# Sketched attention and a SwiGLU block on one core: other chunks of the output product in parts, alternating accumulator banks, and the main sum copied out one unit ahead

## The chip, the core and the metric

One core of a Trainium2 chip runs the whole program. The metric is the device time of one execution in microseconds (us), and for several runs their median. The engines, as the profile names them: PE is the matrix engine and PEld its weight loads, DVE the vector engine, ACT the scalar engine, POOL GpSimd, SP the engine that issues most of the DMAs.

## The reference

Inputs are float32. Attention comes first, with polynomial features of two small sketches; its output, heads side by side, is the input of a SwiGLU block.

```python
# q, k, v: (4, 4, 1088, 32)  S1, S2: (8, 32)
phi(x) = outer(S1 x, S2 x)                    # 64 features
kv = sum over s of phi(k) v;  z = sum over s of phi(k)
attn = (phi(q) kv) / (phi(q) z + 1e-6)
x = attn as (4352, 128)
g = x @ w_gate;  val = x @ w_val              # (4352, 1536)
out = (g * sigmoid(g) * val) @ w_out          # (4352, 128)
```

## The kernel before, in words

**Blocks and chunks.** The 4352 tokens are cut into ten blocks (`blocks`, L65 to L72): blocks 0 to 2 are batch 0 (384, 384 and 320 tokens), blocks 3 to 8 have 480 tokens and block 9, the last, has 384. The 1536 hidden channels are 12 chunks (NCH) of 128. A unit (i, j) is chunk j of block i: its gate and value products, SiLU, and the product of the two, the hidden tile. The down product adds, for each block, 12 chunks of hidden times w_out into one bank of PSUM, and `store` (L1091) turns the sum by 32x32 squares on DVE and sends it out with DMAs on SP's queue.

**The main loop.** Blocks 3 to 9 (`line`, L887) are 84 units, run by the loop at L1339 with y as the unit's number; in these texts block 3 + k, chunk j is written k.j, so y = 12k + j. Attention of the later batches is a generator (`attentions`, L608), advanced by `parts_of` once a unit up to y = 19; its groups of matmuls stand at y = 4, 6, 20, 22 and 40 (`GROUPS`). Every engine runs its instructions in the order in which the code issues them. Nothing reorders them, so the order of the calls is the schedule.

**Products in parts.** From block 3 on, a product is made from two parts of each operand: `cut_unit` (L959) multiplies a difference part into one bank (L968), and the main parts into another (L978, L979). ACT copies the first with a scale (L972) to SBUF, and DVE adds the second to it (L980, `sum`). Up to y = 19 only the value product is made so; from y = 20 (`GATES`) both are, side by side in a pair of banks. SiLU (L986) and POOL's product (L991) of a unit are then issued one unit late, by `finish`.

**Parts of tokens.** `cut_tokens` (L867) makes the parts of a block of tokens: x1 on ACT (L875) and x0 on POOL (L876) in its first step, xd on DVE (L880) in its second. `token_steps` (L1329) says at the end of which unit each step is issued. Block 3 + m needs them from y = 12m.

**The down product in parts.** Blocks 6, 7 and 8 (`line[3:6]`) multiply every third chunk (`DOWN`, L888) in parts as well: `cut_hidden` (L929) makes h1 on ACT, h0 on POOL and hd on DVE (L945), 2, 3 and 4 units after the unit. `down` (L1039) then issues three matmuls (L1052 into the block's bank, L1054 and L1055 into a second bank, "p"), where a plain chunk takes one matmul (L1058, in two passes). The other chunks of these blocks use w_out scaled by -4096 (`scaled`), so that the whole sum is p (1 + 1/4096) - d / 4096, where d is the block's bank. `put_together` (L1068) makes it: an ACT copy of d one unit after the block's last chunk, a DVE sum of the two after two units, the store after three. `before` and `behind` hold such steps by unit: `before` is run after a unit's ACT copy, `behind` after SiLU of the unit before it; both stand ahead of the unit's own `sum`.

**Banks and the queue of downs.** PSUM has 8 banks. Bank 3 ("acc") is held back all the time, bank 2 ("g2") from y = 20 on; the other six are taken as three pairs in turn, two pairs a unit. d of blocks 5 to 9 lies in g2, p always in acc. Units that are done wait in `todo`; `down` is called when it holds more than 5, or more than 6 ahead of the first chunk of blocks 4 and 7 to 9 (`wait`, L1352). So at y = 54, 66 and 78 there is no down, and at y = 55, 67 and 79 there are two.

Of the kernel before, what the change touches and what calls it, by code (L numbers as in the profile page):

```python
# [7 lines left out]
FP32 = mybir.dt.float32  # L8
# [4 lines left out]
AF = mybir.ActivationFunctionType  # L13
ALU = mybir.AluOpType
# [5 lines left out]
def kernel(  # L20
# [28 lines left out]
    nc = tc.nc  # L49
    P = nc.NUM_PARTITIONS  # L50
# [8 lines left out]
    NCH = Dff // P  # L59
# [11 lines left out]
    WB = 480  # L71
# [12 lines left out]
    fpool = ctx.enter_context(tc.tile_pool(name="ffn", bufs=2))  # L84
# [13 lines left out]
    def touch(*which):  # L98
        for i in which:
            clock[0] += 1  # L100
            used[i] = clock[0]
# [11 lines left out]
    def bank(tag=None):  # L113

        if tag is not None:
            i = place[tag]
        elif oldest[0]:
            i = min((i for i in used if i not in held), key=used.get)
        else:
            i = place[free_banks[turn[0] % len(free_banks)]]  # L120
            turn[0] += 1
        touch(i)
        return PS[:, i, :]
# [21 lines left out]
    wo = const.tile([P, NCH, D], FP32, name="wo")  # L145
# [32 lines left out]
    def load_next():  # L178
# [36 lines left out]
        out=ident[:], in_=ident[:], pattern=[[-1, P]], base=0, channel_multiplier=1,  # L215
# [583 lines left out]
    acc = {}  # L799
    todo = []  # L800
# [9 lines left out]
    BETA = 4096.0  # L810
# [4 lines left out]
    def whole(ap):  # L815
        return ap.bitcast(FP32)
# [50 lines left out]
    def cut_tokens(i, engine=nc.gpsimd):  # L867

        t0, n = blocks[i]
        x = xT[:, t0 : t0 + n]  # L870
        x1, x0, xd = x_parts[i] = [
            apool.tile([P, WB], F32R, tag=tag, name=name, bufs=2)
            for tag, name in (("qb", "x1"), ("dT", "x0"), ("rd", "xd"))
        ]
        nc.scalar.activation(x1[:, 0:n], x, AF.Copy, scale=CUT)  # L875
        engine.tensor_tensor(  # L876
            out=x0[:, 0:n], in0=x, in1=whole(x1[:, 0:n]), op=ALU.subtract
        )
        yield
        nc.vector.scalar_tensor_tensor(  # L880
            out=xd[:, 0:n], in0=whole(x0[:, 0:n]), scalar=-BETA, in1=whole(x1[:, 0:n]),
            op0=ALU.mult, op1=ALU.add,
        )
# [1 line left out]


    line = list(range(HEAD, len(blocks)))  # L887
    DOWN = [(i, j) for i in line[3:6] for j in range(2, NCH, 3)]  # L888
    down_parts = {}
    h_parts = {}  # L890
    h_sets = []
    before, behind = {}, {}

    def add_to(where, y, f):
        where.setdefault(y, []).append(f)
# [5 lines left out]
    def cut_down():  # L901

        n = NCH // 3
        parts = const.tile([P, 3, n, D], F32R, tag="late", name="dparts", bufs=1)
        w1, wb, wd = (parts[:, k] for k in range(3))
        scaled = apool.tile([P, n, 2, D], FP32, tag="zs", name="scaled")
        low = [apool.tile([P, 2, D], FP32, tag=tag, name="low" + tag)[:] for tag in ("kas", "kab2")]
        down_parts.update(w1=w1, wb=wb, wd=wd, scaled=scaled)
        third = wo[:, 2::3, :]
        others = wo[:].rearrange("p (c t) d -> p c t d", t=3)[:, :, 0:2, :]  # L910
        cs = [slice(c, c + 2) for c in range(0, n, 2)]
        nc.scalar.activation(w1, third, AF.Copy, scale=CUT)
        yield
        for c, x in zip(cs, low):
            nc.gpsimd.tensor_tensor(
                out=x, in0=third[:, c], in1=whole(w1[:, c]), op=ALU.subtract
            )
            yield
        for c, x in zip(cs, low):
            nc.scalar.activation(wb[:, c], x, AF.Copy, scale=BETA)  # L920
        yield
        for c in cs:
            nc.gpsimd.tensor_tensor(
                out=wd[:, c], in0=whole(w1[:, c]), in1=whole(wb[:, c]), op=ALU.subtract
            )
            yield
        nc.scalar.activation(scaled[:], others, AF.Copy, scale=-BETA)
# [31 lines left out]
    def cut_unit(i, j, both=False, y=None):  # L959
# [24 lines left out]
        def last():  # L984
# [6 lines left out]
            nc.gpsimd.tensor_tensor(out=hj[:, 0:n], in0=sg, in1=sums[:, len(ws) - 1], op=ALU.mult)  # L991
            if (i, j) in DOWN:
                cut_hidden(y, i, j)
# [45 lines left out]
    def down(y=None):  # L1039

        i, j = todo.pop(0)
        n = SPLIT if i == LAST else blocks[i][1]
        if j == 0:
            acc[i] = bank("g1" if i == 1 else "g2" if i in line[2:] else "acc")
        mine = [c for c in range(NCH) if (i, c) in DOWN]
        if mine and j == mine[0]:
            acc[i, "p"] = bank("acc")
        sides = dict(start=(j == 0), stop=(j == NCH - 1))
        if j in mine:
            w1, wb, wd = [down_parts[x][:, j // 3, :] for x in ("w1", "wb", "wd")]  # L1050
            h1, h0, hd = h_parts.pop((i, j))
            nc.tensor.matmul(acc[i][:, 0:n], wd, hd, **sides)  # L1052
            p = acc[i, "p"][:, 0:n]
            nc.tensor.matmul(p, w1, h1, start=(j == mine[0]), stop=False)  # L1054
            nc.tensor.matmul(p, wb, h0, start=False, stop=(j == mine[-1]))  # L1055
        else:
            w = down_parts["scaled"][:, j // 3, j % 3, :] if mine else wo[:, j, :]
            nc.tensor.matmul(acc[i][:, 0:n], w, hidden[i, j][:, 0:n], **sides)  # L1058
        if i != LAST:
            hidden.pop((i, j))  # L1060
            slots.append(slot_of[i, j])
        if j == NCH - 1:
            if mine:
                put_together(y, i, n)
            else:
                store(i, n)

    def put_together(y, i, n):  # L1068

        s = fpool.tile([P, WB], FP32, tag="sg", name="sum2", bufs=5)[:, 0:n]  # L1070
        d, p = acc.pop(i)[:, 0:n], acc.pop((i, "p"))[:, 0:n]
        acc[i] = s
        add_to(behind, y + 1, lambda: nc.scalar.activation(s, d, AF.Copy, scale=-1.0 / BETA))
        add_to(before, y + 2, lambda: nc.vector.scalar_tensor_tensor(
            out=s, in0=p, scalar=1.0 + 1.0 / BETA, in1=s, op0=ALU.mult, op1=ALU.add
        ))
        add_to(before, y + 3, lambda: store(i, n))

    def straight(ps, j):

# [10 lines left out]
    def store(i, n):  # L1091
        t0 = blocks[i][0]

        o = fpool.tile([P, WB // 32, 32], FP32, tag="o", name="o", bufs=2)
        nc.vector.transpose(
            out=o[:, 0 : n // 32, :], in_=acc.pop(i)[:, 0:n].rearrange("p (x t) -> p x t", t=32)
        )
        t1 = t0 + n
        while t0 < t1:
            b, x0 = divmod(t0 // 32, NX)  # L1100
            m = min(t1 - t0, S * (b + 1) - t0) // 32
            k = (t0 - blocks[i][0]) // 32
            for a in range(4):
                queue = nc.scalar if i == LAST and a % 2 else nc.sync
                queue.dma_start(
                    out=rows[b, a, :, x0 : x0 + m, :],
                    in_=o[32 * a : 32 * a + 32, k : k + m, :],
                )
            t0 += 32 * m
# [18 lines left out]
    for h in range(H):  # L1128
# [13 lines left out]
        out=s12[:],  # L1142
        in0=sTv.unsqueeze(1).to_broadcast([P, H, 2, R]),
        in1=own[:].unsqueeze(2).unsqueeze(3).to_broadcast([P, H, 2, R]),
# [20 lines left out]
    n = steps[0][1]  # L1165
# [58 lines left out]
    def group():  # L1224
        while ahead[0] != "pe":
            ahead[0] = next(att)
        ahead[0] = next(att, "end")
# [32 lines left out]
    w = ("wg", "wv")  # L1260
# [10 lines left out]
    for z, (i, j) in enumerate(seq):  # L1271
# [16 lines left out]
        if z == 20:  # L1288
# [4 lines left out]
            first, low, second, third = cut_weights(wv, lows, nc.gpsimd)  # L1293
# [32 lines left out]
    END = len(line) * NCH  # L1326
# [2 lines left out]
    token_steps = {}  # L1329
    for m, i in enumerate(line[1:], 1):  # L1330
        gen = cut_tokens(i)
        for at in {2: (20, 22), 4: (40, 43)}.get(m, (NCH * m - 9, NCH * m - 7 if m > 3 else NCH * m - 4)):
            token_steps.setdefault(at, []).append(gen)
    oldest[0] = True
    hold("acc")
# [3 lines left out]
    for y in range(END):  # L1339
        i, j = line[y // NCH], y % NCH  # L1340
        if y in GROUPS:
            group()
        if y == GATES:
            hold("g2")
        if y == END - 1:
            finish()
            unit(i, j)
        else:
            cut_unit(i, j, both=y >= GATES, y=y)
        for _ in range(2):  # L1350

            wait = todo[0][1] == 0 and todo[0][0] in line[1:2] + line[4:]  # L1352
            if len(todo) > min(5 + wait, END - y + 1):
                down(y)
        parts_of(y < GATES or y % 2 == 0)
        if y == 0:
            gate_rows = cut_weights(wg, lows, nc.vector)
        for n, row in enumerate(gate_rows):
            if y >= (0, 2, 6, 6)[n]:
                take(row, 1)  # L1360
        for gen in token_steps.get(y, ()):
            next(gen, None)
        if y in range(24, 38, 2):
            next(down_steps, None)
# [43 lines left out]
```

## Time and profile before

| | |
|---|---|
| median of 5 runs | 287.66 us (287.48 to 288.49) |
| the profiled execution's own time | 287.73 us |
| its span (first to last instruction) | 286.0 us |
| granted PE clock | 1.0 throughout |
| busy: DVE / ACT / POOL | 221.0 / 175.2 / 176.4 us |
| plain down chunk, 480 tokens, on PE | 0.81 us |
| DVE `sum` of a unit, one product / both | 0.65 / 1.16 us |
| DVE xd (L880), 7 times | 0.65 to 1.65 us |
| POOL product of a unit (L991), 480 tokens | 1.21 us at the shortest |
| DVE sum in `put_together` (L1074), 3 times | 0.64 us |
| ACT copy in `put_together` (L1073), 3 times | 0.57 us |

Times in the views count from the span's start. The main loop begins with the matmul at 93.26 us, y = 20 is at about 140 us, y = 54 at 218, y = 66 at 244, y = 78 at 268. "Idle before" in brackets is the time for which an engine stood still ahead of an instruction, with what released it.

### The profile page before, as it was taken

What the parts mean: (1) busy time and instruction counts of PE and PEld (TensorE: products, weight loads), DVE (VectorE), ACT (ScalarE), POOL (GpSimd) and SP (SyncE); (2) the same over time, 40 slices, a digit from 0 to 9 for tenths busy, and PEclk for the clock granted to TensorE, in tenths of its full rate; (3) what the DMA queues carried; (4) which work ended last, traced back from release to release, by engine and by line L of the source; (5) the groups of instructions that cost most, each with busy time, mean ns of one, the idle gap of its engine ahead of it and who ended that gap; (6) DMA issues with size and microseconds to landing.
All of it is one profiled execution on the core that took longest, in us unless ns stands there. A gap on an engine that the chain in (4) does not pass through costs nothing.

```text
span 286.0 us, 5579 instructions
## 1 busy us (share of the span) xinstructions
PE 278.3 (97%) x2129; PEld 190.8 (67%) x2129; DVE 221.0 (77%) x324; ACT 175.2 (61%) x316; POOL 176.4 (62%) x173
## 2 busy tenths in 40 slices
PE   8899999999999999999999999999999999999995
PEld 7545565666665675655676767757777677778884
DVE  3997988975595977999658889649887987888751
ACT  3568665723401857555276786867788688877760
POOL 3315432279500895499735878649979678888560
PEclk9999999999999999999999999999999999999999
DMA  6474194222321133001000020002000200020021
GB/s 199 153 217 115 55 263 138 80 78 80 89 33 28 26 91 83 2 0 26 12 16 0 1 34 2 0 2 34 0 0 1 36 1 0 1 37 1 0 34 28
DMA packets 26138, 14.28 MB, mean 50 GB/s; under 512 B 19840, under 2 KB 24192, under 8 KB 26112
## 3 DMA queue, kind: packets, MB, share of 16 engines
q1 hardware_dynamic: 25456, 13.84, 18.8%
q8 instruction: 16, 0.26, 0.4%
q10 hardware_dynamic: 656, 0.10, 0.2%
q14 instruction: 10, 0.08, 0.1%
HBM read 11.41 MB, written 2.23 MB: 48 GB/s over the span
## 4 chain that ended last, share of the span: by engine, by line
PE 86%; DVE 7%; ACT 2%; issue 2%; DMA 1%; SPq 0%; DVEq 0%; ACTq 0%
PE PS L1058 24%; PE PS L1015 16%; PE PS L968 10%; PE PS L978 10%; PE PS L979 10%; PE PS L970 5%; DVE sum L980 2%; PE PS L776 2%; PE PS L335 2%; PE PS L347 1%; DMA kld<-in_k_dram 1%; PE PS L381 1%; PE PS L1081 1%; ACT sum L972 1%; PE PS L1055 1%
## 5 line engine op out<-in xcount | busy, mean ns | idle before, releaser
L991 POOL TENSOR_TENSOR hbuf<-sg,sum 128x480 f32<-128x480 f32 (+1 forms) x83 | 105.2, 1272 | 39.9 <-ACT sg L986 32.5
L980 DVE SCALAR_TENSOR_TENSOR sum<-PS,sum 128x960 f32<-128x960 f32 (+2 forms) x83 | 83.3, 1004 | 29.9 <-ACT sum L972 24.0
L972 ACT ACTIVATE sum<-PS 128x960 f32<-128x960 f32 (+2 forms) x83 | 71.0, 855 | 39.1 <-PE PS L968 37.2
L1058 PE MATMUL PS<-hbuf,wo 128*128 128x480 f32 (+3 forms) x142 | 57.5, 506 | 0.0
L968 PE MATMUL PS<-xd,gphq 128*128 128x480 f32 (+1 forms) x63 | 39.1, 620 | 1.2 <-DVE sum L980 0.7
L978 PE MATMUL PS<-x,w 128*128 128x480 f32 (+1 forms) x83 | 38.5, 464 | 0.0
L986 ACT ACTIVATE sg<-sum 128x480 f32<-128x480 f32 (+1 forms) x63 | 36.7, 582 | 2.9 <-DVE sum L980 2.8
L968 PE MATMUL PS<-xd,wd 128*128 128x480 f32 (+1 forms) x83 | 35.8, 432 | 0.5 <-DVE xd L880 0.5
L1058 PEld LDWEIGHTS PS<-hbuf,wo 128*128 128x128 f32 x142 | 26.5, 189 | 8.7 <-issue 0.9
L979 PE MATMUL PS<-x,wb 128*128 128x480 f32 (+1 forms) x83 | 31.2, 376 | 0.0
L1015 PE MATMUL PS<-xT,wg 128*128 128x384 f32 (+1 forms) x74 | 29.5, 480 | 0.0
L1015 PE MATMUL PS<-xT,wv 128*128 128x384 f32 (+1 forms) x74 | 28.8, 471 | 0.2 <-DVE wv L279 0.2
L1019 ACT ACTIVATE sg<-PS 128x384 f32<-128x384 f32 (+1 forms) x31 | 14.4, 467 | 21.3 <-PE PS L1015 19.6
L968 PEld LDWEIGHTS PS<-xd,wd 128*128 128x128 f32 x83 | 15.7, 189 | 12.7 <-issue 11.3
L978 PE MATMUL PS<-x,graw 128*128 128x480 f32 (+1 forms) x63 | 23.8, 378 | 0.2 <-ACT xT L793 0.2
L979 PE MATMUL PS<-x,graw 128*128 128x480 f32 (+1 forms) x63 | 23.3, 371 | 0.0
L1058 PE MATMUL PS<-hbuf,scaled 128*128 128x480 f32 x48 | 23.1, 570 | 0.0
L968 PEld LDWEIGHTS PS<-xd,gphq 128*128 128x128 f32 x63 | 11.9, 188 | 12.3 <-issue 6.6
L1015 PEld LDWEIGHTS PS<-xT,wv 128*128 128x128 f32 x74 | 13.8, 190 | 9.2 <-DVE hbuf L1030 0.9
L1015 PEld LDWEIGHTS PS<-xT,wg 128*128 128x128 f32 x74 | 13.3, 189 | 9.3 <-issue 1.2
L978 PEld LDWEIGHTS PS<-x,w 128*128 128x128 f32 x83 | 15.6, 188 | 5.8 <-issue 3.2
L979 PEld LDWEIGHTS PS<-x,wb 128*128 128x128 f32 x83 | 15.6, 188 | 5.7 <-issue 4.3
(173 smaller groups left out, 457.3 us busy)
## 6 DMA issues: line engine op xcount, KB each, us to landing
kld<-in_k_dram SPq DMA_DIRECT2D x4, 544.0 KB, 4.1
vld<-in_v_dram SPq DMA_DIRECT2D x12, 144.0 KB, 5.5
qld<-in_q_dram SPq DMA_DIRECT2D x3, 544.0 KB, 3.5
raw<-in_moe_w_out_dram SPq DMA_DIRECT2D x4, 384.0 KB, 4.7
raw<-in_moe_w_gate_dram SPq DMA_DIRECT2D x3, 384.0 KB, 3.2
raw<-in_moe_w_val_dram SPq DMA_DIRECT2D x3, 384.0 KB, 3.4
out_dram<-o SPq DMA_DIRECT2D x16, 60.0 KB, 2.0
vld<-in_v_dram SPq DMA_DIRECT2D x4, 112.0 KB, 4.3
```

Source lines behind the costliest of these rows:

```text
L335: nc.tensor.matmul(ps[32 * a : 32 * a + 32, 96 * (c - c0) : 96 * (c - c0) + 96], qT[:, 4 * c + a, :], s123[:, a : a + H, :, :].rearrange(" ...
L968: nc.tensor.matmul(ds[:, k], wd, xd, start=True, stop=True)
L970: nc.tensor.matmul(g, wg[:, j, :], xT[:, t0 : t0 + n], start=True, stop=True)
L972: nc.scalar.activation(sums, ds, AF.Copy, scale=-1.0 / BETA)
L978: nc.tensor.matmul(ps[:, k], w1, x1, start=True, stop=False)
L979: nc.tensor.matmul(ps[:, k], wb, x0, start=False, stop=True)
L980: nc.vector.scalar_tensor_tensor(out=sums, in0=ps, scalar=1.0 + 1.0 / BETA, in1=sums, op0=ALU.mult, op1=ALU.add)
L986: nc.scalar.activation(sg, sums[:, 0] if both else g, AF.Silu)
L991: nc.gpsimd.tensor_tensor(out=hj[:, 0:n], in0=sg, in1=sums[:, len(ws) - 1], op=ALU.mult)
L1015: nc.tensor.matmul(o[:, 0:n], w[:, j, :], xT[:, t0 : t0 + n], start=True, stop=True)
L1019: nc.scalar.activation(sg[:, 0:n], g[:, 0:n], AF.Silu)
L1058: nc.tensor.matmul(acc[i][:, 0:n], w, hidden[i, j][:, 0:n], **sides)
```

## The change

1. The chunks in parts are 1, 4, 7, 10 in place of 2, 5, 8, 11, with the matching slices of w_out. The last chunk of a block is then a plain one.
2. d and p change places from block to block: blocks 5, 7 and 9 keep d in g2 (7 has p in acc), blocks 6 and 8 have d in acc and p in g2.
3. p is copied out, scaled, by ACT one unit after chunk 10 (`copy_out`). DVE adds d to it one unit after chunk 11, and the store follows one unit later.
4. The extra unit of waiting ahead of the first chunk of blocks 7 to 9 goes; that of block 4 stays.
5. The token steps move: block 4's from y = 3 and 8 to y = 2 and 3, block 7's from 40 and 43 to 40 and 42, block 8's from 51 and 53 to 50 and 51, block 9's from 63 and 65 to 62 and 63. Those of blocks 5 and 6 stay.

```diff
-    DOWN = [(i, j) for i in line[3:6] for j in range(2, NCH, 3)]
+    DOWN = [(i, j) for i in line[3:6] for j in range(1, NCH, 3)]
...
-        third = wo[:, 2::3, :]
-        others = wo[:].rearrange("p (c t) d -> p c t d", t=3)[:, :, 0:2, :]
+        third = wo[:, 1::3, :]
+        others = wo[:].rearrange("p (c t) d -> p c t d", t=3)[:, :, 0::2, :]
...
-            acc[i] = bank("g1" if i == 1 else "g2" if i in line[2:] else "acc")
+            acc[i] = bank("g1" if i == 1 else "g2" if i in line[2::2] else "acc")
...
-            acc[i, "p"] = bank("acc")
+            acc[i, "p"] = bank("acc" if i in line[2::2] else "g2")
...
+            if j == mine[-1]:
+                copy_out(y, i, n)
         else:
-            w = down_parts["scaled"][:, j // 3, j % 3, :] if mine else wo[:, j, :]
+            w = down_parts["scaled"][:, j // 3, j % 3 // 2, :] if mine else wo[:, j, :]
...
+    def copy_out(y, i, n):
+
+        x = fpool.tile([P, WB], FP32, tag="sg", name="sum2", bufs=5)[:, 0:n]
+        p = acc[i, "p"][:, 0:n]
+        acc[i, "p"] = x
+        add_to(behind, y + 1, lambda: nc.scalar.activation(x, p, AF.Copy, scale=1.0 + 1.0 / BETA))
+
     def put_together(y, i, n):
 
-        s = fpool.tile([P, WB], FP32, tag="sg", name="sum2", bufs=5)[:, 0:n]
-        d, p = acc.pop(i)[:, 0:n], acc.pop((i, "p"))[:, 0:n]
-        acc[i] = s
-        add_to(behind, y + 1, lambda: nc.scalar.activation(s, d, AF.Copy, scale=-1.0 / BETA))
-        add_to(before, y + 2, lambda: nc.vector.scalar_tensor_tensor(
-            out=s, in0=p, scalar=1.0 + 1.0 / BETA, in1=s, op0=ALU.mult, op1=ALU.add
+        d, x = acc.pop(i)[:, 0:n], acc.pop((i, "p"))
+        acc[i] = x
+        add_to(before, y + 1, lambda: nc.vector.scalar_tensor_tensor(
+            out=x, in0=d, scalar=-1.0 / BETA, in1=x, op0=ALU.mult, op1=ALU.add
         ))
-        add_to(before, y + 3, lambda: store(i, n))
+        add_to(before, y + 2, lambda: store(i, n))
...
-        for at in {2: (20, 22), 4: (40, 43)}.get(m, (NCH * m - 9, NCH * m - 7 if m > 3 else NCH * m - 4)):
+        for at in {2: (20, 22), 3: (27, 32), 4: (40, 42)}.get(m, (NCH * m - 10, NCH * m - 9)):
...
-            wait = todo[0][1] == 0 and todo[0][0] in line[1:2] + line[4:]
-            if len(todo) > min(5 + wait, END - y + 1):
+            if len(todo) > min(5 + (todo[0] == (line[1], 0)), END - y + 1):
```

## The prediction

> **What bounds the kernel now.** I read part 1 of the page and the head of part 4 first: PE is busy 97% of the span and is 86% of the chain that ended last.
>
> ```profile
> PE 278.3 (97%) x2129; PEld 190.8 (67%) x2129; DVE 221.0 (77%) x324; ACT 175.2 (61%) x316; POOL 176.4 (62%) x173
> ...
> PE 86%; DVE 7%; ACT 2%; issue 2%; DMA 1%; SPq 0%; DVEq 0%; ACTq 0%
> ```
>
> The change alters no PE work: per chunk in parts three matmuls before and after, per plain chunk two passes. So only stalls of PE can be won or lost. A busy row hides them, so I laid the chain of waits against the matmul work. Steady pieces, from the chain's rows: first products 0.435 us, main products 0.866 (four at 0.216), a plain down 0.81, one in parts 0.645. From 196.02 (y = 43) to 217.12 (y = 53) that makes 21.06 us of work in 21.10: PE is full there. Not so at the first block transition, where the chain leaves PE:
>
> ```profile
> 216.67 0.45 PE PS L968 x2
> ...
> 217.20 0.99 ACT sum L972
> ...
> 218.26 1.16 DVE sum L980
> 219.42 0.54 DVE xd L880
> 219.96 0.95 issue
> 220.91 0.45 DVE hvld L945
> 221.36 0.62 issue
> ...
> 222.50 1.16 DVE sum L980
> ...
> 223.69 0.70 PE PS L968 x2
> ...
> 225.91 0.43 PE PS L968 x2
> ```
>
> (Columns: start, us, what.) From 217.12 to 225.91, 8.79 us, the work is 5.73 (to the first products of y = 56) plus 1.95 (that unit): 7.68. **Lost: 1.11 us.** Why, in the timelines of DVE and POOL:
>
> ```profile
> 219.34 1.65 DVE L880 SCALAR_TENSOR_TENSOR xd<-x,x 128x480 fp32r<-128x480 f32 x1
> 220.91 1.66 DVE L945 SCALAR_TENSOR_TENSOR hvld<-hvld,hqld 128x480 fp32r<-128x480 f32 x1
> 222.50 1.15 DVE L980 SCALAR_TENSOR_TENSOR sum<-PS,sum 128x960 f32<-128x960 f32 x1
> 223.56 0.64 DVE L1074 SCALAR_TENSOR_TENSOR sum<-PS,sum 128x480 f32<-128x480 f32 x1
> ```
>
> ```profile
> 219.23 1.25 POOL L991 TENSOR_TENSOR hbuf<-sg,sum 128x480 f32<-128x480 f32 x1
> 220.69 1.36 POOL L991 TENSOR_TENSOR hbuf<-sg,sum 128x480 f32<-128x480 f32 x1 [0.22 <-ACT sg L986]
> ```
>
> xd and hd stand back to back (y = 53, 54), each held by a POOL product until that ends (220.48, 222.05) and done about 0.51 later. The sum of y = 54 starts 4.24 us after that of y = 53; PE, with no down at y = 54 to fill the time, waits for its banks. The same sum elsewhere gives 0.17 us at y = 66 (244.39 to 248.78, 4.39 for 4.22), 0.36 at y = 78 (267.73 to 271.05, 3.32 for 2.96), and 0.25 at y = 42 (193.66 to 196.02, 2.36 for 2.11), where the first down of block 6 waits until DVE has turned block 5's sum out of g2 (194.16 + 0.67). **In all 1.89 us.**
>
> **What the Trainium skill says.** "SBUF — State Buffer", "Who interferes with whom": a DVE instruction with two SBUF inputs and a GpSimd one that reads SBUF exclude each other for the whole instruction, whoever issues first. The trace agrees: xd takes 0.65 us with POOL idle (117.00), 1.65 above. The `sum`s read PSUM and SBUF and keep 1.16. "PSUM — Partial Sum Buffer", "PSUM bank collisions": guard PSUM by the bank. So a bank's next user waits for its last reader; the 0.25 us at y = 42 is such a wait.
>
> **The change, part by part.** The queues follow from the code's order.
>
> *Chunks, banks, copy-out, downs.* Each block has one ACT copy (0.57), one DVE sum (0.64), one turn (0.67) as before, and four DMA issues on SP (1.9 us a store), alone in that queue there: no count changes. Each unit at a transition now has its down, so PE is given 0.81 (or 0.645) us where it had none. Block 7's first chunk goes to g2, read last by the copy a unit before; the copy reads p, complete since chunk 10. Block 6 starts in acc, long free. So all three rows of wait lose their cause, as does y = 42's.
>
> *Is the DVE pile-up gone?* xd of block 8 goes to the end of y = 51, hd to y = 50, 53, 56, DVE's sum to 54, the turn to 55. Moving the rows of before by the units: xd waits for POOL until 218.1 and ends 218.6, so the next sum is 0.35 late; hd ends 221.0, its sum 0.8 late; the unit after 0.4, then 0.1. What is allowed: from the end of a unit's products to the next use of that pair PE has a down, 1.30, a down: 2.92, less 0.44 until ACT's copy lets the sum begin, 1.16 for it and 0.04: **1.28 us**. All within. Block 9's xd is shorter (384 tokens, 1.38 at 245.11). Block 7's at y = 42 keeps a unit free ahead of hd at 44: I get 1.0 late. I leave 0.1 us for one miss; bounds 0 and 1.2 (the losses stay at y = 54 and 66, shifted). **Gain 1.8.**
>
> *Block 4's xd from y = 8 to y = 3.* This is the dear one. In DVE's queue it lands behind the L865 row at 101.24 and ahead of attention's fold, and it must wait for x0, which POOL has behind three unit products:
>
> ```profile
> 101.24 0.99 DVE L865 TENSOR_TENSOR late<-wg,graw 128x384 f32<-128x384 f32 x1
> 102.15 0.21 DVE L594 TENSOR_TENSOR fold<-PS,sq 128x64 f32<-128x64 f32 x1
> ...
> 102.71 0.67 DVE L601 TENSOR_TENSOR s<-w,own 128x64 f32<-128x64 f32 x1
> 103.30 0.24 DVE L723 STREAM_TRANSPOSE spread<-PS 128x64 f32<-128x64 f32 x1
> ```
>
> ```profile
> 98.42 0.74 POOL L540 TENSOR_TENSOR zs<-zs,phk 128x256 f32<-128x256 f32 x1
> ...
> 103.26 1.21 POOL L991 TENSOR_TENSOR hbuf<-sg,sum 128x480 f32<-128x480 f32 x1
> 104.43 1.58 POOL L876 TENSOR_TENSOR x<-xT,x 128x480 fp32r<-128x480 f32 x1
> ```
>
> ```profile
> 105.90 1.48 PEld L335 LDWEIGHTS PS<-s,qT 128*32 128x32 f32 x72 [0.71 <-issue]
> ```
>
> The fourth product stands at 103.26; x0 takes its place, and at 1.21 us (192.29, undisturbed) ends at 104.47. Before, DVE was free at 102.23. POOL goes straight on with the fourth product, to 105.65, and by the lock xd ends 0.51 later, 106.16. Then fold to turn: 1.11 us undisturbed (142.36 to 143.47), so 107.25. Behind them stand the sums of y = 4 and 5. PE's L335 (attention's sketches, y = 6) needs `s`, and the bank that L723 reads: it starts at 107.3, not 105.90. **Cost 1.4 us**, all on PE, for PE is in order. The cover that it had was 105.9 - 103.54 = 2.4 us, and the shift of L723 (3.7) eats it. What follows is no later: sums 4 and 5 are done by about 109, the sum of y = 6 was at 109.38 after 2.96 us of DVE idle. The 0.65 us that leave y = 8 are worth nothing, as PE did not wait there. x1 a unit earlier delays ACT by 0.6 us, ahead of a DVE sum that starts only at 100.67: nothing. The spread DMAs on SP start 3.7 us later and are read at y = 20, 35 us on.
>
> **Sum:** 287.73 - 1.8 + 1.4 = 287.3 for the profiled execution; from the median, 287.66, the same 287.3.
>
> **Rivals.** *A*, the forecast, 287.3, with 0.3 to 0.4 either way: 286.9 to 287.7. *B*, DVE gets the lock at 104.5 ahead of the fourth product: xd to 105.15, but `s` has two SBUF inputs and waits for that product, to 106.4; L335 at 106.75; cost 0.85, time 286.7. For it: nothing shows who wins when POOL's next instruction is ready; against: POOL's rows follow with no gap. *C*, **slower**: DVE's wait at y = 3 is longer. With x0 at its recorded end (106.0, DVE disturbing it), xd at its longest (1.65) and fold to turn as recorded (1.39), L335 starts at 109.1: cost 3.2, time 289.1. It decides from a cost of 2.4, L723 ending after 108.3. Against it: DVE stands still meanwhile and can't disturb POOL. *D*: the pile-up only moves, to y = 53 or 44, where hd follows one unit after xd: gain 1.2 at most, time 287.5 to 288.2. For it: the lock makes each take 1.4 to 1.66. Against: y = 45 of before has the same spacing and shows no loss. That the change doesn't do what it says, I can exclude: the queues are as the code issues them.
>
> **The numbers.** A 0.55, B 0.20, D 0.15, C 0.10. A measurement can tell about 0.2% (0.58 us) from no change. Faster by that: B, and some two fifths of A: 0.42. Slower: C and a third of D: 0.15. Within: 0.43. The range leaves out C and little else: 286.4 (B with the whole 1.89) to 288.2 (D).
>
> **What will show it.** Right: DVE idle from about 102.2 until 104.5 or later ahead of xd, L335 at about 107.3 and PE idle ahead of it; from y = 40 on no chain through DVE at y = 54 to 56, no wait of L1058 for an ACT copy; POOL otherwise as before. Wrong: L335 at its old place (then about 285.9), or PE idle of a microsecond at y = 53 to 57.

## The result and the profile after

The changed kernel takes 287.09 us (median of 31 runs), the kernel before 287.87 us (median of 52 beside them): ratio 0.9972, 95% interval 0.9960 to 0.9983. The profiled execution took 286.87 us against 287.73, its span 285.0 us against 286.0. The forecast was 0.4 us less; it is 0.8.

The page's PE row and the head of its chain:

```profile
PE 276.7 (97%) x2129; PEld 191.0 (67%) x2129; DVE 221.0 (78%) x324; ACT 175.5 (62%) x316; POOL 177.4 (62%) x173
...
PE 89%; DVE 5%; DMA 1%; ACT 1%; POOL 1%; issue 1%; SPq 0%; DVEq 0%; ACTq 0%
```

The same 2129 matmuls, a smaller DVE share of the chain. At the first block transition, where the chain left PE before, it now stays on PE (chain of waits at y = 53 to 56; start, us, what):

```profile
217.23 0.44 PE PS L968 x2
...
218.53 0.81 PE PS L1060 x2
219.33 0.44 PE PS L968 x2
...
220.65 0.81 PE PS L1060 x2
221.45 0.44 PE PS L968 x2
...
222.75 0.22 PE PS L1052
...
223.41 0.43 PE PS L968 x2
```

Every unit there now has its down (L1060 is what L1058 was), and no matmul waits: 2.10 to 2.12 us from one L968 to the next with a plain down, 1.96 with one in parts. DVE's timeline shows xd and hd with a sum between them, then the joining sum (L1081, DVE's sum of d and p):

```profile
215.77 1.46 DVE L880 SCALAR_TENSOR_TENSOR xd<-x,x 128x480 fp32r<-128x480 f32 x1
217.16 1.15 DVE L980 SCALAR_TENSOR_TENSOR sum<-PS,sum 128x960 f32<-128x960 f32 x1
218.37 1.65 DVE L945 SCALAR_TENSOR_TENSOR hvld<-hvld,hqld 128x480 fp32r<-128x480 f32 x1
219.94 1.14 DVE L980 SCALAR_TENSOR_TENSOR sum<-PS,sum 128x960 f32<-128x960 f32 x1
221.01 0.64 DVE L1081 SCALAR_TENSOR_TENSOR sum<-PS,sum 128x480 f32<-128x480 f32 x1
```

The other side is at y = 3 to 6. DVE and POOL there:

```profile
101.09 0.99 DVE L865 TENSOR_TENSOR late<-wg,graw 128x384 f32<-128x384 f32 x1
104.36 1.65 DVE L880 SCALAR_TENSOR_TENSOR xd<-x,x 128x480 fp32r<-128x480 f32 x1 [2.27 <-POOL x L876]
105.93 0.21 DVE L594 TENSOR_TENSOR fold<-PS,sq 128x64 f32<-128x64 f32 x1
...
106.48 0.22 DVE L601 TENSOR_TENSOR s<-w,own 128x64 f32<-128x64 f32 x1
106.62 0.24 DVE L723 STREAM_TRANSPOSE spread<-PS 128x64 f32<-128x64 f32 x1
```

```profile
103.11 1.21 POOL L876 TENSOR_TENSOR x<-xT,x 128x480 fp32r<-128x480 f32 x1
104.28 1.21 POOL L991 TENSOR_TENSOR hbuf<-sg,sum 128x480 f32<-128x480 f32 x1
```

DVE stands still for 2.27 us, until POOL has x0. Then xd is held by the product that POOL began 0.08 us ahead of it; this exclusion, which the prediction describes, is called the lock from here on. L335 gets its operands late (PE's waits; columns: who waited for whom, us in total, times, longest):

```profile
PE PS L335 <- DVE spread L723: 1.1, 1, 1.1
```

**Where the time went, by stretches of units.** I took the start of each unit's second L968 (its only one up to y = 19) from PE's timeline. For the stretches from y = 42 on the table gives the time lost: length less matmul work (1.301 us a unit at 480 tokens and 1.05 at 384, 0.81 a plain down, 0.645 one in parts, 0.43 one of the last block). For the others it gives the length, since the work is the same.

| stretch | before | changed | no token moves (e5) | only tokens of 7 to 9 (e6) |
|---|---|---|---|---|
| y = 4 to 6, length | 5.53 | 6.70 | 5.53 | 5.54 |
| y = 7 to 20, length | 33.03 | 33.04 | 33.03 | 33.03 |
| y = 22 to 24, length | 5.00 | 5.00 | 4.99 | 4.99 |
| y = 42 to 47, lost | 0.25 | 0.0 | 0.0 | 0.25 |
| y = 53 to 57, lost | 1.14 | 0.0 | 0.72 | 0.28 |
| y = 65 to 69, lost | 0.19 | 0.0 | 0.42 | 0.19 |
| y = 77 to 81, lost | 0.37 | 0.0 | 0.0 | 0.37 |

So the change wins 1.95 us and pays 1.17: from the first matmul of the main loop to the start of DVE's last instruction, 189.25 us (93.26 to 282.51) became 188.42 (93.11 to 281.53), 0.83 less. The remaining 0.15 us of the two spans lie ahead of the loop, where nothing was changed.

### The profile page after: what moved, and what is told of

Its sections match the earlier page's. It is cut to its first block, busy times and chain, and to the rows that moved or that the text cites. A ratio compares the mean times of both kernels' runs of the same rounds, so it can differ in the third digit from the quotient of the medians.

```text
span 285.0 us, 5583 instructions
## 1 busy us (share of the span) xinstructions
PE 276.7 (97%) x2129; PEld 191.0 (67%) x2129; DVE 221.0 (78%) x324; ACT 175.5 (62%) x316; POOL 177.4 (62%) x173
## 4 chain that ended last, share of the span: by engine, by line
PE 89%; DVE 5%; DMA 1%; ACT 1%; POOL 1%; issue 1%; SPq 0%; DVEq 0%; ACTq 0%
PE PS L1060 24%; PE PS L1015 16%; PE PS L968 11%; PE PS L978 10%; PE PS L979 10%; PE PS L970 5%; PE PS L776 2%; PE PS L335 2%; PE PS L347 2%; PE PS L381 2%; DMA kld<-in_k_dram 1%; DVE xd L880 1%; PE PS L1088 1%; PE PS L1055 1%; PE PS L1054 1%; PE PS L1052 1%
## 5 line engine op out<-in xcount | busy, mean ns | idle before, releaser
L1060 PE MATMUL PS<-hbuf,wo 128*128 128x480 f32 (+3 forms) x142 | 57.5, 505 | 0.0
L968 PE MATMUL PS<-xd,gphq 128*128 128x480 f32 (+1 forms) x63 | 40.1, 636 | 0.5 <-DVE xd L880 0.5
L968 PE MATMUL PS<-xd,wd 128*128 128x480 f32 (+1 forms) x83 | 35.8, 432 | 0.5 <-DVE xd L880 0.5
L1060 PEld LDWEIGHTS PS<-hbuf,wo 128*128 128x128 f32 x142 | 26.6, 189 | 8.4 <-issue 0.9
L968 PEld LDWEIGHTS PS<-xd,wd 128*128 128x128 f32 x83 | 15.7, 189 | 13.1 <-issue 11.4
L1060 PE MATMUL PS<-hbuf,scaled 128*128 128x480 f32 x48 | 23.2, 564 | 0.0
L968 PEld LDWEIGHTS PS<-xd,gphq 128*128 128x128 f32 x63 | 11.9, 188 | 11.7 <-issue 6.8
```

The source lines that it names most:

```text
L968: nc.tensor.matmul(ds[:, k], wd, xd, start=True, stop=True)
```

## The experiments

The theory after the result: **(T)** the down product's new steps and the moved token steps of blocks 7 to 9 clear the transitions (1.95 us), and block 4's xd at y = 3 costs 1.17 us, by DVE's wait for x0 and by the exclusion of xd by POOL's next product. Rivals: the cost at y = 3 is covered or has another cause; xd waits for x0 alone and the lock plays no part; the moved tokens alone, or the downs alone, make the gain. Ratios are to the kernel before, run on the same chip, with 95% intervals.

**e1: the change without its move of block 4's steps.**

```diff
-{2: (20, 22), 3: (27, 32), 4: (40, 42)}.get(m, (NCH * m - 10, NCH * m - 9))
+{1: (3, 8), 2: (20, 22), 3: (27, 32), 4: (40, 42)}.get(m, (NCH * m - 10, NCH * m - 9))
```

> The changed kernel with one part undone: the token steps of block 4 stand at y = 3 and 8 again. Theory (DVE's wait for x0 at y = 3 costs PE 1.15 us, read from L335 at 106.92 in place of 105.8): 1.15 us under the changed kernel, about 285.9, L335 with no wait ahead of it. Rival (the wait is covered later, the whole gain is what the profile shows and no more): the same as the changed kernel, 287.1.

285.87 us, ratio 0.9913 (0.9890 to 0.9937). y = 4 to 6 takes 5.54 us again, every other stretch is as in the changed kernel, and xd, x0 and L335 stand where they stood before. So the move of block 4's steps is the cost, and it is not given back later.

**e2: that move alone, on the kernel before.**

```diff
-{2: (20, 22), 4: (40, 43)}.get(m, ...)
+{1: (2, 3), 2: (20, 22), 4: (40, 43)}.get(m, ...)
```

> The kernel before with that one part alone: token steps of block 4 at y = 2 and 3. Theory: 1.15 us above the kernel before, about 289.0 (ratio 1.004). Rival (it costs only together with the new downs, or is covered): as before, 287.9.

289.34 us, ratio 1.0042 (1.0028 to 1.0056), some 1.2 us. y = 4 to 6: 6.70. The part stands for itself: alone it makes the kernel slower, by 1.17 us there, where the prediction had 1.4.

**e3: x0 one POOL product later, xd where the change has it.**

```diff
+{1: (3, 3), 2: (20, 22), 3: (27, 32), 4: (40, 42)}.get(m, ...)
```

> The changed kernel with block 4's steps both at y = 3: x0 stands behind the fourth POOL product, xd where it is. Theory with the lock (in the changed kernel xd has to wait for the fourth product anyway, and here nothing runs on POOL when x0 is done): L335 only 0.25 us later, the time 0.25 us above the changed kernel, xd at 0.65 us. Rival (xd waits for x0 alone, and its 1.65 us are not the fourth product's): x0 ends 1.2 us later, so L335 and the time 1.2 us later, about 288.3, xd at 1.65 us still.

287.28 us, ratio 0.9972 (0.9961 to 0.9982): as the changed kernel. y = 4 to 6: 6.88, 0.18 more. DVE's and POOL's rows:

```profile
105.91 0.66 DVE L880 SCALAR_TENSOR_TENSOR xd<-x,x 128x480 fp32r<-128x480 f32 x1 [3.43 <-POOL x L876]
```

```profile
104.67 1.20 POOL L876 TENSOR_TENSOR x<-xT,x 128x480 fp32r<-128x480 f32 x1
108.11 1.39 POOL L991 TENSOR_TENSOR hbuf<-sg,sum 128x480 f32<-128x480 f32 x1 [2.23 <-DVE sum L980]
```

Counted from the start of the main loop, which is 0.39 us later in this trace, x0 ends 1.2 us later than in the changed kernel, yet L335 starts only 0.18 later: with nothing after x0 on POOL, xd takes 0.66 us, not 1.65. The rival without a lock is out.

**e4: x0 one POOL product earlier.**

```diff
+{1: (1, 3), 2: (20, 22), 3: (27, 32), 4: (40, 42)}.get(m, ...)
```

> The changed kernel with block 4's steps at y = 1 and 3: x0 stands behind the second POOL product. Theory with the lock: x0 ends at about 103.1, but xd waits for the third product, to 104.3 and 0.5 more, and L601 for the fourth; L335 at about 106.4, the time 0.55 us under the changed kernel. Rival (no lock): xd at 103.2 with 0.65 us, all of it in the cover of 2.4 us, the time 1.15 us under the changed kernel.

286.49 us, ratio 0.9933 (0.9909 to 0.9956). y = 4 to 6: 5.99, 0.71 less than the change and 0.45 over e1. Both of DVE's operations with two SBUF inputs are held by a product:

```profile
103.75 1.65 DVE L880 SCALAR_TENSOR_TENSOR xd<-x,x 128x480 fp32r<-128x480 f32 x1 [1.10 <-POOL x L876]
...
105.88 0.67 DVE L601 TENSOR_TENSOR s<-w,own 128x64 f32<-128x64 f32 x1
```

**e8: the fourth product on DVE, so that POOL has nothing after x0.**

```diff
+            engine = nc.vector if (i, j) == (line[0], 3) else nc.gpsimd
-            nc.gpsimd.tensor_tensor(out=hj[:, 0:n], in0=sg, in1=sums[:, len(ws) - 1], op=ALU.mult)
+            engine.tensor_tensor(out=hj[:, 0:n], in0=sg, in1=sums[:, len(ws) - 1], op=ALU.mult)
```

> The changed kernel with the fourth product of the main loop (block 3, chunk 3) on DVE in place of POOL, so that nothing on POOL follows x0. Theory with the lock: xd takes 0.65 us in place of 1.65, L335 starts at about 106.0 and waits 0.15 us, the time 1.0 us under the changed kernel. Rival (the length of xd has another cause, or the product's 0.6 us on DVE come on top): 0.3 us under it at most.

286.56 us, ratio 0.9937 (0.9915 to 0.9958). y = 4 to 6: 6.13, so 0.57 us less than the change, between the two expectations. The lock's part holds, xd takes 0.66 us:

```profile
102.27 1.56 DVE L865 TENSOR_TENSOR late<-wg,graw 128x384 f32<-128x384 f32 x1
104.93 0.66 DVE L880 SCALAR_TENSOR_TENSOR xd<-x,x 128x480 fp32r<-128x480 f32 x1 [1.10 <-POOL x L876]
```

```profile
103.38 1.52 POOL L876 TENSOR_TENSOR x<-xT,x 128x480 fp32r<-128x480 f32 x1
```

What I had missed: the product on DVE pushes L865 back, which then has the lock to 103.83 and holds x0, 1.52 us in place of 1.21. Moving an operation off POOL changed who held whom. Counted from the start of the main loop, x0 ends 0.41 us later than in the changed kernel and xd 0.59 sooner, so the lock was worth the whole 1.0 us by which xd is shorter.

**e5: the new down product, all token steps as before.**

```diff
-{2: (20, 22), 3: (27, 32), 4: (40, 42)}.get(m, (NCH * m - 10, NCH * m - 9))
+{2: (20, 22), 4: (40, 43)}.get(m, (NCH * m - 9, NCH * m - 7 if m > 3 else NCH * m - 4))
```

> The changed kernel with all token steps where they were before (the chunks, banks, copy-out and downs stay new). Theory (the steps of the down product alone take most of the pile-up away; xd at the end of y = 53 then stands next to the joining sum in place of hd, so 0.2 to 0.3 us stay): about 286.2, 0.9 us under the changed kernel, with little idle of PE at y = 54 to 56. Rival (the moved token steps are what clears the transition): the 1.1 us of y = 54 stay, 287.0.

287.23 us, ratio 0.9964 (0.9950 to 0.9978). My expectation failed: 0.72 us stay at y = 53 to 57, and at y = 65 to 69 the loss rises from 0.19 to 0.42, together about as much as block 4's move costs. The traces of DVE and POOL:

```profile
217.59 1.65 DVE L945 SCALAR_TENSOR_TENSOR hvld<-hvld,hqld 128x480 fp32r<-128x480 f32 x1 [0.56 <-POOL hvld L942]
219.17 1.14 DVE L980 SCALAR_TENSOR_TENSOR sum<-PS,sum 128x960 f32<-128x960 f32 x1
220.24 0.64 DVE L880 SCALAR_TENSOR_TENSOR xd<-x,x 128x480 fp32r<-128x480 f32 x1
```

```profile
215.13 1.22 POOL L876 TENSOR_TENSOR x<-xT,x 128x480 fp32r<-128x480 f32 x1
216.32 1.24 POOL L942 TENSOR_TENSOR hvld<-hbuf,hqld 128x480 fp32r<-128x480 f32 x1
217.52 2.79 POOL L991 TENSOR_TENSOR hbuf<-sg,sum 128x480 f32<-128x480 f32 x2
```

h0 stands straight behind x0 on POOL (x1 and h1 fall into one unit on ACT as well), so DVE waits for it and then for the product behind it. What is late is hd and the sum at 219.17, ahead of xd; the next experiment tries this.

**e9: e1 with xd of blocks 7, 8 and 9 back at y = 43, 53 and 65, x1 and x0 as in the change.**

```diff
+{1: (3, 8), 2: (20, 22), 4: (40, 43)}.get(m, (NCH * m - 10, NCH * m - 7) if m > 3 else (27, 32))
```

> The new down product with block 4's steps at y = 3 and 8, and for blocks 8 and 9 the first token step where the change has it (y = 50, 62) but xd where it was before (53, 65); block 7's at 40 and 43. It tells what kept 0.7 us at y = 54 in the run without any token moves. Theory (there x1 and h1 fell into one unit on ACT, and h0 stood straight behind x0 on POOL, so hd and the sums came late; xd beside the joining sum is harmless): the stretch from y = 53 to 57 takes 8.3 to 8.5 us, the whole 0.1 to 0.3 us more than with block 4's steps back alone, about 286.1. Rival (xd beside the joining sum on DVE is the cause): 9.0 us, the whole 287.0.

286.02 us, ratio 0.9935 (0.9911 to 0.9958). y = 53 to 57 takes 8.29 us, as in the changed kernel, nothing lost. The difference to e5 is x1 and x0 of blocks 8 and 9 a unit earlier and nothing else, so with the new downs these are what counts of the moved token steps, and xd may stay beside the joining sum. Whether ACT's or POOL's meeting of the two weighs more was not tried.

**e6: only the token steps of blocks 7 to 9, on the kernel before.**

```diff
-{2: (20, 22), 4: (40, 43)}.get(m, (NCH * m - 9, NCH * m - 7 if m > 3 else NCH * m - 4))
+{1: (3, 8), 2: (20, 22), 3: (27, 32), 4: (40, 42)}.get(m, (NCH * m - 10, NCH * m - 9))
```

> The kernel before with the token steps of blocks 7, 8 and 9 moved as in the change, all else as before (block 4's steps too). Theory (xd and hd no longer meet on DVE): 1.0 us of the 1.28 at y = 54 and 66 go, the 0.25 at y = 42 and the 0.36 at y = 78 stay; ratio 0.9965 to before. Rival (it is the missing down at y = 54 and the double one at 55 that make PE wait): as before, or 0.2 us less.

287.12 us, ratio 0.9965 (0.9953 to 0.9978). y = 53 to 57 loses 0.28 us in place of 1.14; y = 65 to 69 keeps its 0.19, y = 42 and 78 theirs. So 0.86 us go in place of the expected 1.0, all at y = 54. That it was xd against hd there is read from the trace of before, where hd does not wait for h0; e6 moves x1, x0 and xd together and can't tell them apart. The small wait at y = 66 was something else. I take it for the missing down and the copy on ACT, as at y = 78; no run tries that alone. Of the 1.14 us at y = 53 to 57 the downs alone win 0.42 (e5) and the token steps alone 0.86, and together they win it all.

**e7: e1 with block 5's xd at y = 21.**

```diff
-{1: (3, 8), 2: (20, 22), 3: (27, 32), 4: (40, 42)}.get(m, ...)
+{1: (3, 8), 2: (20, 21), 3: (27, 32), 4: (40, 42)}.get(m, ...)
```

> The changed kernel with block 4's steps at y = 3 and 8 again and block 5's xd at the end of y = 21 in place of 22. Theory (in every trace so far PE waits at y = 24 for block 5's xd, which stands behind attention's dot on DVE, while DVE is idle for 2.8 us after the sum of y = 21): PE's wait of 0.5 us for xd there and a late start go, 0.6 us under the run with block 4's steps back, about 285.3. Rival (the sum of y = 22 or the banks hold PE there as well): 285.9.

285.47 us, ratio 0.9907 (0.9880 to 0.9933). y = 22 to 24: 4.22 us in place of 5.00, all else as in e1. That is the matmul work of two units with plain downs (2 x 2.11), so PE's wait for xd at y = 24 is gone whole; xd now fills time in which DVE had nothing.

**e10, e11, e12: the changed kernel, e1 and e7 side by side on one chip.**

> The changed kernel as it is, to stand beside the next two on one chip: 0.8 us under the kernel before, 287.1.

> The changed kernel with block 4's steps at y = 3 and 8, on the same chip as the changed kernel. Theory: 1.15 us under it, ratio to the kernel before 0.993. Rival (the 1.2 us between medians of two calls were the chips'): 0.5 us or less under it.

> The same with block 5's xd at y = 21 too, on the same chip. Theory: 0.75 us under the run with block 4's steps back, as the stretch from y = 22 to 24 fell from 5.00 to 4.22 us; ratio to before 0.9905. Rival (the 0.75 us are given back after y = 24): the same as with block 4's steps back alone.

287.00 us, ratio 0.9973 (0.9960 to 0.9986); 286.08 us, 0.9937 (0.9915 to 0.9960); 285.22 us, 0.9911 (0.9886 to 0.9936). The medians differ by 0.92 and 0.86 us where 1.15 and 0.75 were expected; the stretches are those of the earlier runs within 0.02 us. In the kernel before, block 5's xd stood at 151.77, behind the dot (L741) at 150.35. DVE in e12:

```profile
145.35 1.16 DVE L980 SCALAR_TENSOR_TENSOR sum<-PS,sum 128x960 f32<-128x960 f32 x1 [0.15 <-ACT sum L972]
146.43 1.22 DVE L880 SCALAR_TENSOR_TENSOR xd<-x,x 128x480 fp32r<-128x480 f32 x1
149.30 1.16 DVE L980 SCALAR_TENSOR_TENSOR sum<-PS,sum 128x960 f32<-128x960 f32 x1 [1.65 <-ACT sum L972]
150.37 1.01 DVE L741 TENSOR_TENSOR dot<-qab 128x288 f32<-128x288 f32 x1
```

e7 and e12 are one kernel, 0.9% under the kernel before and 0.6% under the changed one: the fastest version tried.

## Why the prediction was right, step by step

**Only stalls can move.** Right: same matmuls, and from y = 42 on the changed kernel loses nothing that the table can show.

**The gain, 1.8 us.** 1.95 measured. The four places and their sizes hold (0.25, 1.11, 0.17, 0.36 forecast as lost before; 0.25, 1.14, 0.19, 0.37 by the second reckoning), and all went to zero. The 0.1 us kept back for a miss at y = 44 was not needed. The forecast put hd's end 2.4 us after xd's (218.6 and 221.0), and in the trace it is 2.8 (217.2 and 220.0, both a microsecond or more sooner). The sum after hd began 1.2 us after ACT's copy for it was done (218.73 to 219.94), where the forecast had 0.8 us and could allow 1.28: it held, but only just. One reason was too narrow: I named xd against hd and took y = 66 for the same case. e6 shows that y = 66 kept its 0.19 us with the tokens moved. And I credited the spacing of xd, where e5 and e9 show that under the new downs it is x1 and x0 coming a unit sooner. That the change moved them too is luck as far as the forecast goes: it reckoned nothing for them.

**The cost of block 4's steps, 1.4 us.** Right in mechanism, place and sign, 1.17 in size. Seen from the start of the main loop (0.15 us earlier in this trace), x0's row ended at 104.47 and xd's at 106.16, both as forecast. Two small terms were too large: fold began at 106.08, ahead of the end of xd's row, and from fold (L594) to the end of the turn (L723) it took 0.93 us, not the 1.11 of y = 20, mostly because the turn's row here begins before that of L601 ends. So L335 began at 107.07, not 107.3.

The lock came as forecast (e3, e8), and rival B, DVE first, is out: POOL began the next product 0.04 us before x0's row ended, and xd was issued 0.08 us after that. Rival C needed x0 at 106.0 and did not come: x0 took 1.21 us, for DVE stood still. In e8, where DVE was at work, it did take 1.52.

The wait and the lock are not two shares of the 1.17 us. DVE's wait of 2.27 us and a short xd would almost have fitted into the cover, the 2.4 us that lay before between the turn and L335. By an estimate from e8, where the lock was worth 1.0 us, L335 would then have been some 0.2 us late. So with the wait given, nearly all that PE pays is the product that POOL began just before xd could go; without the wait (e1) there is no cost at all.

**What follows is no later.** Right: y = 6 to 20 is the same within 0.02 us in all traces, though DVE was 3 us behind at y = 4.

**The other rivals and the range.** D: the pile-up neither stayed nor moved in the changed kernel. In e5 it did stay, through POOL and ACT. B: by the time alone it would have fitted better than the forecast, 1.0 us of gain against 0.4, with 0.8 measured; only the trace tells them apart. For B the text says that nothing shows who wins when POOL's next instruction is ready. For a DVE operation that already waits, the trace of before does show it: hd at 226.83 ended 0.5 us after the running product, and POOL's next one, begun at 227.98, took 1.57 us. At y = 3 xd waited not for the lock but for its data, and the product was first. One sum of the range is off: B with the whole 1.89 us is 286.6, not 286.4.

**The sum.** -1.95 + 1.17 = -0.78, and the medians say -0.78. The forecast of -0.4 was half of it, by 0.15 us of gain and 0.23 of cost. Both errors went the same way, so they added up; the time, 287.09, lies in the lower half of the forecast's 286.9 to 287.7. A gain of over 0.58 us had been put at 0.42, no more likely than one that can't be told from nothing (0.43).

## What to carry to other kernels

An operation issued earlier in an in-order queue pulls all that is behind it into its wait: look up when its last input will be there, and who is behind, before moving it ahead. Where operations of two engines exclude each other, as here, moving one changes the length of others, so count in the product that starts just before a wait ends: here, by the estimate above, it was 1.0 us of a cost of 1.17. Compare stretches between fixed matmuls of the traces: here they agree to 0.02 us where the whole program's times scatter by 1 us.

## What the runs showed that I had not expected

Between the traces, the spans spread ahead of the main loop. In the twelve experiments' and the two kernels' traces its first matmul starts between 93.03 and 94.55 us, while each stretch after it repeats within some 0.02 us where the code is the same. e6's profiled execution, 288.17 us, is 1 us over its median, and its loop starts 1.3 us later than that of the kernel before. Another part of the spread lies outside the span: e7's profiled execution took 287.07 us with a span of 283.8, e12's, of the same kernel, 285.14 with 283.3. Why either varies was not studied.

A waiting DVE operation went ahead of POOL's next one. In the changed kernel hd was issued at 218.37, while POOL ran:

```profile
216.67 1.67 POOL L942 TENSOR_TENSOR hvld<-hbuf,hqld 128x480 fp32r<-128x480 f32 x1
218.30 1.21 POOL L991 TENSOR_TENSOR hbuf<-sg,sum 128x480 f32<-128x480 f32 x1
...
219.47 1.64 POOL L991 TENSOR_TENSOR hbuf<-sg,sum 128x480 f32<-128x480 f32 x1
```

The first of the two products ended at 219.51. hd ended at 220.02, 0.5 us after that, and it was POOL's next product, begun at 219.47, that was held: 1.64 us in place of 1.21. The row of h0 at 216.67 shows the same behind xd. It holds in all fourteen traces: of 266 rows of xd and hd with 384 or 480 tokens, 226 started while a POOL operation had more than 0.06 us to run, and each of these ended 0.4 to 0.6 us after that one operation; the other 40 took 0.65 us.
